# One block of p·v per pair of heads in every second unit, instead of half a block in every unit

## The chip, the core and the metric

One Trainium2 chip, one of its cores. The metric is the device time of one execution in microseconds (us). Each of the core's engines runs its own instructions in order: TensorE (PE, its weight loads apart as PEld), VectorE (DVE), ScalarE (ACT), GpSimd (POOL), and SyncE (SP), which here only issues DMAs. They meet at semaphores.

## What is computed

Attention in which a query sees only the keys of its own hash bucket, then a mixture of experts with a capacity for each expert, then a gated layer behind an RMS norm. The change lies in the attention, here for batch 2, 8 heads, 768 positions and 64 columns:

```python
mask = q_bucket[:, :, :, None] == k_bucket[:, :, None, :]
scores = scale * np.matmul(q, k.transpose(0, 1, 3, 2))
scores = np.where(mask, scores, -1000000000.0)
scores = scores - np.max(scores, axis=-1, keepdims=True)
attn = np.exp(scores)
attn = attn / (np.sum(attn, axis=-1, keepdims=True) + 1e-09)
return np.matmul(attn, v).astype(np.float32)
```

## The kernel before

The attention works on eight pairs of heads (`p`), each pair on six tiles of 128 queries. A block `i` is one tile of one pair; it has two units, u = 2i and u = 2i + 1, one for each head. So a pair takes 12 units, and the whole loop runs over u = 0 to 98, with 96 units of real work. In this text u0 is the first unit of a pair (12, 24, ...), and "relative unit 10" is u0 + 10.

The order is written out by hand, and every engine keeps to it. In unit u:

- `expo(u + 1)`: ACT takes the exponential of a score tile out of PSUM (L342), with the row sum.
- `transp(u)`: PE transposes the exponentials in two halves of three 128x128 pieces (L353); DVE or ACT copies each half to SBUF as `pt` (L357, L355).
- `scores(u + 2)`: four matmuls on PE (L328, L331); DVE then takes the minimum of each row (L333) and makes two scalars of it (L334, L335). The exponential two units on waits for them.
- even u from 4: `comb(i)` on PE (L387) and `comb_v(i)` on DVE (L409 to L416) for the block that was finished in the unit before.
- odd u from 3: `rinv`, three small DVE instructions for the reciprocals of the row sums (L396, L397).
- from u = 2: `pv(u // 2 - 1, u % 2)`. Six matmuls (L372), half of the 12 of a block: chunks 0 to 2 of the keys in the even unit, 3 to 5 in the odd one. Each has 64 columns of weights, one head writing to the upper and one to the lower 64 partitions of `xo`. Behind the second half ACT copies `xo` to SBUF as `xt` (L377), which `comb` reads in the next unit.
- last the `fill` of this unit.

The fill lists prepare the next pair of heads and convert weights for the later layers. For the next pair: `prep_t` (PE transposes, L272; ACT copies, L276 or L278; POOL splits into a high and a low part, L279 and L280) for the halves of k in the fills of relative units -1 and 0, and of q in those of 1 and 3. `prep_d` issues six DMAs on SP for k and six for q, behind the POOL work. `prep_p` (12 matmuls, L288) and `prep_s` (four DMAs, L313) stand in relative unit 7. The scores of the next pair start in relative unit 10.

A weight conversion `conv(n)` stands in relative units 0, 2, 5, 7 and 9: one ACT instruction, two on DVE (L247, L248) and four on POOL (L249 to L252, about 4.5 us of POOL together). Its output `ha` has three buffers, so L247 of one conversion waits until the store of the third before it has landed. The store (`conv_store`, L257) stands on SP four units behind the conversion. So the store of the conversion of relative unit 0 stands on SP behind the `prep_d` of q (relative unit 3), and it frees the buffer that the conversion of relative unit 7 writes.

After the attention come the routing, the experts (layers 1 and 2) and the gated layer. They don't overlap with the attention's loop, apart from weights that are loaded ahead.

Of the kernel before, what the change touches and what calls it, by code (L numbers as in the profile page):

```python
# [9 lines left out]
F32 = mybir.dt.float32  # L10
# [6 lines left out]
AF = mybir.ActivationFunctionType  # L17
# [26 lines left out]
def lsh_attention__moe__swiglu_kernel(ctx, tc, q, k, v, proj, m_wg, m_w1, m_w2,  # L44
                                      f_wg, f_wv, f_wo, f_g, out):
    nc = tc.nc
# [6 lines left out]
    TPB = S // 128  # L53
# [28 lines left out]
    wk = att.enter_context(tc.tile_pool(name="wk", bufs=2))  # L82
    cv = att.enter_context(tc.tile_pool(name="cv", bufs=2))
    ps_s = att.enter_context(tc.tile_pool(name="ps_s", bufs=2, space=PSUM))
    ps_v = att.enter_context(tc.tile_pool(name="ps_v", bufs=1, space=PSUM))
# [229 lines left out]
    SC, PR, PTT, RS, XO = {}, {}, {}, {}, {}  # L315

    def scores(u):
        i, h = divmod(u, 2)
        p, t = divmod(i, TPB)
        k1, k2 = STK["k", p]  # L320
        q1, q2 = STK["q", p]
        if h == 0:
            RS[i] = wk.tile([128, 2, 4], F32, name="rs", bufs=4)
        rs = RS[i]
        ps = ps_s.tile([128, 2, 512], F32, name="sc")
        qs = slice(t * 128, (t + 1) * 128)
        for n in range(2):
            nc.tensor.matmul(ps[:, n, :HALF], q1[:, h, qs], k1[:, h, n * HALF:(n + 1) * HALF],  # L328
                             start=True, stop=False)
        for n in range(2):  # L330
            nc.tensor.matmul(ps[:, n, :HALF], q2[:64 + NS, h, qs], k2[:64 + NS, h, n * HALF:(n + 1) * HALF],  # L331
                             start=False, stop=True)
        nc.vector.tensor_reduce(rs[:, h, 0:1], ps[:, :, :HALF], axis=AX.XY, op=OP.min)  # L333
        nc.vector.tensor_scalar(rs[:, h, 1:2], rs[:, h, 0:1], BIG / 2, -1.0, op0=OP.is_lt, op1=OP.mult)  # L334
        nc.vector.tensor_scalar(rs[:, h, 2:3], rs[:, h, 0:1], BIG / 2, rs[:, h, 0:1], op0=OP.is_lt, op1=OP.mult)  # L335
        SC[u] = ps

    def expo(u):
        i, h = divmod(u, 2)
        rs, ps = RS[i], SC.pop(u)  # L340
        pt = wk.tile([128, 2, HALF], F32, name="pr", bufs=3)
        nc.scalar.activation(pt, ps[:, :, :HALF], AF.Exp, scale=rs[:, h, 1:2], bias=rs[:, h, 2:3],  # L342
                             accum_out=rs[:, h, 3:4])
        PR[u] = pt

    def transp(u):
        pt = PR.pop(u).rearrange("p a b -> p (a b)")
        o = wk.tile([128, TPB, 128], F32, name="pt", bufs=4)
        for half in range(2):
            t = ps_m.tile([128, 512], F32, name="m")[:, :HALF].rearrange("p (c k) -> p c k", c=3)  # L350
            for i in range(3):
                c = half * 3 + i
                nc.tensor.transpose(t[:, i, :], pt[:, c * 128:(c + 1) * 128], ident)  # L353
            if half == 1 or u % 4 < ACT_EVAC:
                nc.scalar.activation(o[:, 3 * half:3 * half + 3, :], t, AF.Copy)  # L355
            else:
                nc.vector.tensor_copy(o[:, 0:3, :], t)  # L357
        PTT[u] = o

    def pv(i, part):  # L360
        p = i // TPB
        vt = LD["v", p]
        if part == 0:
            if i < NU // 2 - 1:
                XO[i] = ps_v.tile([128, 128], F32, name="xo")
            else:
                XO[i] = ps_s.tile([128, 2, 512], F32, name="sc")[:, 0, :128]
        xo = XO[i]
        a = (PTT[2 * i], PTT[2 * i + 1])
        for c in range(3 * part, 3 * part + 3):  # L370
            for h in range(2):
                nc.tensor.matmul(xo[64 * h:64 * h + 64], vt[:, h, c, :], a[h][:, c, :],  # L372
                                 start=(c == 0), stop=(c == TPB - 1))
        if part == 1:
            del PTT[2 * i], PTT[2 * i + 1]
            xt = wk.tile([128, 128], F32, name="xt", bufs=3)
            nc.scalar.activation(xt, xo, AF.Copy)  # L377
            XO[i] = xt

    XS = {}  # L380

# [2 lines left out]
    def comb(i):  # L384
        p, t = divmod(i, TPB)
        pc = ps_m.tile([128, 512], F32, name="m")
        nc.tensor.matmul(pc[:, :2 * W], XO.pop(i), cb[:, p % HP, :], start=True, stop=True)  # L387
        PC[i] = pc
# [3 lines left out]
    def rinv(i):  # L392
        rs = RS.pop(i)
        ri = wk.tile([128, 2, 2], F32, name="ri", bufs=2)
        for h in range(2):
            nc.vector.tensor_scalar(ri[:, h, 0:1], rs[:, h, 3:4], 1e-9, None, op0=OP.add)  # L396
        nc.vector.reciprocal(ri[:, :, 1:2], ri[:, :, 0:1])  # L397
        RI[i] = ri

    def comb_v(i):  # L400
        p, t = divmod(i, TPB)
        b, hp = divmod(p, HP)
        c = b * TPB + t
        ri, pc = RI.pop(i), PC.pop(i)
        if t == 0:
            XS[p] = wk.tile([128, TPB, 2, W], F32, name="xs", bufs=2)
        pcv = pc[:, :2 * W].rearrange("p (h w) -> p h w", h=2)
        if hp == HP - 1:
            nc.vector.tensor_tensor(lp[:, c, 2 * hp:2 * hp + 2, :], pcv[:, :, D:],  # L409
                                    ri[:, :, 1:2].to_broadcast([128, 2, E]), op=OP.mult)  # L410
        if i < NU // 2 - 1:
            nc.vector.tensor_tensor(XS[p][:, t], pcv, ri[:, :, 1:2].to_broadcast([128, 2, W]), op=OP.mult)
        if t == TPB - 1 and hp < HP - 1:
            nc.gpsimd.tensor_copy(lp[:, b * TPB:(b + 1) * TPB, 2 * hp:2 * hp + 2, :], XS[p][:, :, :, D:])
        if hp == HP - 1:
            nc.vector.tensor_reduce(lg[:, c, :], lp[:, c].rearrange("p h e -> p e h"), axis=AX.X, op=OP.add)  # L416
        if i == NU // 2 - 1:
            keys(b)
            for h in range(2):
                nc.scalar.activation(XS[p][:, t, h], pcv[:, h], AF.Copy, scale=ri[:, h, 1:2])  # L420
        if t == TPB - 1:
            for h in range(2):
                nc.sync.dma_start(
                    x_d[b * S:(b + 1) * S, (2 * hp + h) * D:(2 * hp + h + 1) * D].rearrange("(c p) d -> p c d", p=128),
                    XS[p][:, :, h, :D])
            del XS[p]
# [73 lines left out]
    NU = NPAIR * TPB * 2  # L500
# [19 lines left out]
    for n in range(len(convs)):  # L520
        u = CONV + n * 12 // 5
# [71 lines left out]
    for u in range(NU + 3):  # L593

        if u + 1 < NU:
            expo(u + 1)
        if u < NU:
            transp(u)
        if u + 2 < NU:
            scores(u + 2)  # L600
        if u == NU:
            rinv(u // 2 - 1)
            pv(u // 2 - 1, 0)
            pv(u // 2 - 1, 1)
        if u % 2 == 0 and u >= 4:
            comb(u // 2 - 2)
            comb_v(u // 2 - 2)
        if u % 2 == 1 and 3 <= u < NU:
            rinv(u // 2 - 1)
        if 2 <= u < NU:  # L610
            pv(u // 2 - 1, u % 2)
        for f, a in fill.pop(u, []):
            f(*a)
    assert not fill
# [673 lines left out]
```

## Time and profile before

| | us |
|---|---|
| median of three runs | 825.6 (823.95 to 828.76) |
| the profiled execution | 828.43 |
| its span, first to last instruction | 826.3 |
| PE busy over the span | 766.7 |
| the units' loop, first scores to last `comb` | about 16 to 302 |

The loop of units is a third of the time. The granted TensorE clock is given as a share of 2.4 GHz; its mean over the span is 0.961. A time below is a place in the span unless it is plainly a duration.

### The profile page before, as it was taken

What the parts mean: (1) busy time and instruction counts of PE and PEld (TensorE: products, weight loads), DVE (VectorE), ACT (ScalarE), POOL (GpSimd) and SP (SyncE); (2) the same over time, 40 slices, a digit from 0 to 9 for tenths busy, and PEclk for the clock granted to TensorE, in tenths of its full rate; (3) what the DMA queues carried; (4) which work ended last, traced back from release to release, by engine and by line L of the source; (5) the groups of instructions that cost most, each with busy time, mean ns of one, the idle gap of its engine ahead of it and who ended that gap; (6) DMA issues with size and microseconds to landing.
All of it is one profiled execution on the core that took longest, in us unless ns stands there. A gap on an engine that the chain in (4) does not pass through costs nothing.

```text
span 826.3 us, 14742 instructions
## 1 busy us (share of the span) xinstructions
PE 766.7 (93%) x5317; PEld 689.9 (83%) x5317; DVE 524.7 (64%) x1337; ACT 396.5 (48%) x863; POOL 320.9 (39%) x305
## 2 busy tenths in 40 slices
PE   7999989999989973699999998999999999999996
PEld 4788778787877863599988998999999999999995
DVE  7788877888878878478897886665422332233222
ACT  3677666676666770276666764654311211121111
POOL 3287878786777710366665660000100010001001
PEclk7999999999999985699999999999999999999999
DMA  3679989988989424347656824265200110001001
GB/s 77 172 204 232 252 245 242 265 242 240 241 222 256 159 59 128 104 158 260 233 179 196 263 77 130 83 211 151 77 1 1 39 38 1 1 1 39 1 0 39
DMA packets 101744, 113.98 MB, mean 138 GB/s; under 512 B 43820, under 2 KB 74540, under 8 KB 101668
## 3 DMA queue, kind: packets, MB, share of 16 engines
q1 hardware_dynamic: 99588, 106.71, 44.9%
q0 software_dynamic: 1920, 6.29, 2.0%
q8 instruction: 43, 0.70, 0.3%
q14 instruction: 33, 0.27, 0.1%
q10 hardware_dynamic: 160, 0.00, 0.0%
HBM read 76.83 MB, written 18.09 MB: 115 GB/s over the span
## 4 chain that ended last, share of the span: by engine, by line
PE 35%; issue 19%; DVE 2%; DMA 1%; POOL 1%; ACT 1%; SPq 0%; POOLq 0%; another core or an unknown queue 0%; ACTq 0%; DVEq 0%
PE pg L1175 6%; PE pv L1175 6%; PE py L1018 6%; PE po L1203 6%; PE ph L994 5%; PE py L1020 3%; PE ph L996 2%; POOL out_dram L1211 1%; DMA xrow<-x_d,gi 1%; PE ph L972 1%; DMA fraw<-wo_d 1%; DVE wl L212 0%; PE px L1050 0%; DVE yn L1080 0%; DVE xl L954 0%
## 5 line engine op out<-in xcount | busy, mean ns | idle before, releaser
L1211 POOL DMA_INDIRECT out_dram<-ot,oi x12 | 11.7, 975 | 312.3 <-DVE ot L1209 310.6
L342 ACT ACTIVATE pr<-sc,rs 128x768 f32<-128x768 f32 x96 | 95.1, 991 | 61.6 <-DVE rs L335 37.0
L212 POOL TENSOR_TENSOR wl<-wr,wh 128x1024 fp32r<-128x1024 f32 x35 | 84.7, 2428 | 59.3 <-PE ph L972 20.4
L333 DVE TENSOR_REDUCE rs<-sc 128x1 f32<-128x768 f32 x96 | 91.4, 952 | 24.3 <-PE sc L331 24.0
L1184 DVE TENSOR_TENSOR a<-sg,pg 128x384 f32<-128x384 f32 x48 | 26.6, 553 | 103.7 <-ACT sg L1182 103.7
L353 PE MATMUL m<-ident,pr 128*128 128x128 f32 x576 | 84.7, 282 | 6.2 <-ACT pr L342 3.0
L994 PE MATMUL ph<-xg,wh 128*128 128x384 f32 x256 | 78.2, 373 | 8.9 <-DVE ht L1011 8.0
L372 PE MATMUL xo<-pt,ld_v 128*64 128x128 f32 x1128 | 82.8, 282 | 0.0
L353 PEld LDWEIGHTS m<-ident,pr 128*128 128x128 f32 x576 | 62.8, 141 | 20.8 <-issue 6.5
L1018 PE MATMUL py<-ht,wh 128*128 128x384 f32 x256 | 77.2, 365 | 0.0
L372 PEld LDWEIGHTS xo<-pt,ld_v 128*64 128x64 f32 x1128 | 60.0, 137 | 18.6 <-issue 11.9
L1182 ACT ACTIVATE sg<-pg 128x384 f32<-128x384 f32 x48 | 23.5, 489 | 106.2 <-PE pg L1175 106.2
L1188 ACT ACTIVATE ah<-a 128x384 fp32r<-128x384 f32 x48 | 25.2, 525 | 99.0 <-DVE a L1185 99.0
L1175 PE MATMUL pg<-xh,gl 128*128 128x384 f32 x192 | 64.6, 336 | 0.0
L1175 PE MATMUL pg<-xl,gh 128*128 128x384 f32 x192 | 64.5, 336 | 0.0
L1175 PE MATMUL pg<-xh,gh 128*128 128x384 f32 x192 | 64.5, 336 | 0.0
L1175 PE MATMUL pv<-xh,vl 128*128 128x384 f32 x192 | 64.4, 335 | 0.0
L1175 PE MATMUL pv<-xl,vh 128*128 128x384 f32 x192 | 64.4, 335 | 0.0
L1175 PE MATMUL pv<-xh,vh 128*128 128x384 f32 x192 | 64.4, 335 | 0.0
L1020 PE MATMUL py<-ht,wl 128*128 128x192 f32 x256 | 64.0, 255 | 0.0
L355 ACT ACTIVATE pt<-m 128x384 f32<-128x384 f32 x120 | 55.6, 485 | 5.2 <-PE m L353 5.2
L328 PE MATMUL sc<-s_k,s_q 128*128 128x384 f32 x192 | 57.9, 383 | 0.0
(252 smaller groups left out, 1963.0 us busy)
## 6 DMA issues: line engine op xcount, KB each, us to landing
wr<-in_moe_w_dram SPq DMA_DIRECT2D x64, 512.0 KB
w<-in_moe_w_gate_dram SPq DMA_DIRECT2D x12, 512.0 KB
w<-in_moe_w_val_dram SPq DMA_DIRECT2D x12, 512.0 KB
w<-in_moe_w_out_dram SPq DMA_DIRECT2D x12, 512.0 KB
s_k<-nh_k SPq DMA_DIRECT2D x28, 192.0 KB
s_q<-nh_q SPq DMA_DIRECT2D x28, 192.0 KB
ld_k<-in_k_dram SPq DMA_DIRECT2D x16, 192.0 KB
ld_q<-in_q_dram SPq DMA_DIRECT2D x16, 192.0 KB
```

What stands on the lines that cost most here:

```text
L212: (nc.gpsimd if pool else nc.vector).tensor_tensor(WL[i], WR.pop(i), WH[i], op=OP.subtract)
L328: nc.tensor.matmul(ps[:, n, :HALF], q1[:, h, qs], k1[:, h, n * HALF:(n + 1) * HALF], start=True, stop=False)
L333: nc.vector.tensor_reduce(rs[:, h, 0:1], ps[:, :, :HALF], axis=AX.XY, op=OP.min)
L342: nc.scalar.activation(pt, ps[:, :, :HALF], AF.Exp, scale=rs[:, h, 1:2], bias=rs[:, h, 2:3], accum_out=rs[:, h, 3:4])
L353: nc.tensor.transpose(t[:, i, :], pt[:, c * 128:(c + 1) * 128], ident)
L355: nc.scalar.activation(o[:, 3 * half:3 * half + 3, :], t, AF.Copy)
L372: nc.tensor.matmul(xo[64 * h:64 * h + 64], vt[:, h, c, :], a[h][:, c, :], start=(c == 0), stop=(c == TPB - 1))
L994: hi = lambda: nc.tensor.matmul(ph[:, :2 * CAP], wh[:, d], xg[:, d].rearrange("p a b -> p (a b)"), start=(d == 0), stop=(d == KD - 1), ski ...
L1018: hi = lambda: nc.tensor.matmul(py[d][:, :2 * CAP], wh[:, ds], ht[:, f].rearrange("p a b -> p (a b)"), start=(f == 0), stop=(f == KF - 1), ...
L1020: lo = lambda: nc.tensor.matmul(py[d][:, :CAP], wl[:, ds], ht[:, f, 0], start=False, stop=False, skip_group_check=True)
L1175: nc.tensor.matmul(t[:, :TJ], a[:, d, :], b_[:, d, :], start=(n == 0), stop=(n == 3 * KD - 1))
L1203: nc.tensor.matmul(PO[j][t], a[:, ts], b_, start=(f == 0 and n == 0), stop=(f == KG - 1 and n == 2))
```

## The change

A whole block of `pv` (12 matmuls) now runs in every even unit, behind the scores and `comb`; an odd unit has none. The copy `xt` becomes a function of its own, `pv_out`, and runs in the odd unit behind it, on ACT between the exponential and the copies of the transposes. `rinv` moves from the odd to the even unit. The last block runs in u = 96 behind `comb(46)`, where it ran ahead of it. Behind the changed lines all line numbers are smaller by one to four.

```diff
-    def pv(i, part):
+    def pv(i):
...
-        a = (PTT[2 * i], PTT[2 * i + 1])
-        for c in range(3 * part, 3 * part + 3):
+        a = (PTT.pop(2 * i), PTT.pop(2 * i + 1))
+        for c in range(TPB):
             for h in range(2):
                 nc.tensor.matmul(xo[64 * h:64 * h + 64], vt[:, h, c, :], a[h][:, c, :],
                                  start=(c == 0), stop=(c == TPB - 1))
-        if part == 1:
-            del PTT[2 * i], PTT[2 * i + 1]
-            xt = wk.tile([128, 128], F32, name="xt", bufs=3)
-            nc.scalar.activation(xt, xo, AF.Copy)
-            XO[i] = xt
+
+    def pv_out(i):
+        xt = wk.tile([128, 128], F32, name="xt", bufs=3)
+        nc.scalar.activation(xt, XO[i], AF.Copy)
+        XO[i] = xt
...
         if u + 1 < NU:
             expo(u + 1)
+        if u % 2 == 1 and 3 <= u <= NU + 1:
+            pv_out(u // 2 - 1)
         if u < NU:
             transp(u)
         if u + 2 < NU:
             scores(u + 2)
-        if u == NU:
-            rinv(u // 2 - 1)
-            pv(u // 2 - 1, 0)
-            pv(u // 2 - 1, 1)
         if u % 2 == 0 and u >= 4:
             comb(u // 2 - 2)
             comb_v(u // 2 - 2)
-        if u % 2 == 1 and 3 <= u < NU:
+        if u % 2 == 0 and 2 <= u <= NU:
+            pv(u // 2 - 1)
             rinv(u // 2 - 1)
-        if 2 <= u < NU:
-            pv(u // 2 - 1, u % 2)
         for f, a in fill.pop(u, []):
             f(*a)
```

On PE, relative units -1 and 0 of a pair in the middle of the loop, where the next pair's k is transposed (`ld_k`), stand so in the kernel before:

```order
L353 MATMUL m<-ident,pr 128x128 x6
L328 MATMUL sc<-s_k,s_q 128x384 x2
L331 MATMUL sc<-s_k,s_q 128x384 x2
L372 MATMUL xo<-pt,ld_v 64x128 x6
L272 MATMUL m<-ident,ld_k 128x128 x3
L353 MATMUL m<-ident,pr 128x128 x6
L328 MATMUL sc<-s_k,s_q 128x384 x2
L331 MATMUL sc<-s_k,s_q 128x384 x2
L387 MATMUL m<-cb,xt 128x144
L372 MATMUL xo<-pt,ld_v 64x128 x6
L272 MATMUL m<-ident,ld_k 128x128 x3
```

and so in the changed one:

```order
L353 MATMUL m<-ident,pr 128x128 x6
L328 MATMUL sc<-s_k,s_q 128x384 x2
L331 MATMUL sc<-s_k,s_q 128x384 x2
L272 MATMUL m<-ident,ld_k 128x128 x3
L353 MATMUL m<-ident,pr 128x128 x6
L328 MATMUL sc<-s_k,s_q 128x384 x2
L331 MATMUL sc<-s_k,s_q 128x384 x2
L386 MATMUL m<-cb,xt 128x144
L371 MATMUL xo<-pt,ld_v 64x128 x12
L272 MATMUL m<-ident,ld_k 128x128 x3
```

The half block ahead of the first L272 is gone, and the second L272 (the second half of k) stands behind a whole block where it stood behind half of one.

At the end of the loop, PE has in the kernel before (the last block writes to a buffer of `sc`):

```order
L353 MATMUL m<-ident,pr 128x128 x6
L372 MATMUL xo<-pt,ld_v 64x128 x6
L372 MATMUL sc<-pt,ld_v 64x128 x12
L387 MATMUL m<-cb,xt 128x144 x2
L690 LDWEIGHTS reach
```

and in the changed one:

```order
L353 MATMUL m<-ident,pr 128x128 x6
L386 MATMUL m<-cb,xt 128x144
L371 MATMUL sc<-pt,ld_v 64x128 x12
L386 MATMUL m<-cb,xt 128x144
L686 LDWEIGHTS reach
```

Between the last transposes and the last block stands one `comb` now, where half a block of `pv` stood. The order of the DMAs on SP and of the work on POOL is the same in both kernels.

## Rows read from the trace of the kernel before

**Rows 1.** The page: busy time by engine; granted clock in 40 slices.

```profile
PE 766.7 (93%) x5317; PEld 689.9 (83%) x5317; DVE 524.7 (64%) x1337; ACT 396.5 (48%) x863; POOL 320.9 (39%) x305
...
PEclk7999999999999985699999999999999999999999
```

**Rows 2.** Window: length, busy us of PE, PEld, DVE, ACT, POOL; clock, DMA share, GB/s.

```profile
30.00:298.00 268.00, 255.28 (x2295) 215.03 (x2294) 220.72 (x647) 183.94 (x410) 195.61 (x202) 0.99 0.83 228
```

**Rows 3.** Waits in 30 to 305 us: total us, times, longest.

```profile
PE sc L331 <- issue: 4.4, 2, 2.2
```

**Rows 4.** PE in order of time (start, length), units 43 to 45; end of loop.

```profile
151.91 0.82 PE L353 MATMUL m<-ident,pr 128*128 128x128 f32 x6
152.49 0.59 PE L328 MATMUL sc<-s_k,s_q 128*128 128x384 f32 x2
...
153.26 0.41 PE L387 MATMUL m<-cb,xt 128*128 128x144 f32 x2
153.60 0.88 PE L372 MATMUL xo<-pt,ld_v 128*64 128x128 f32 x12
154.41 0.88 PE L353 MATMUL m<-ident,pr 128*128 128x128 f32 x6
155.04 0.59 PE L328 MATMUL sc<-s_k,s_q 128*128 128x384 f32 x2
...
155.92 0.88 PE L372 MATMUL xo<-pt,ld_v 128*64 128x128 f32 x12
...
297.56 0.88 PE L353 MATMUL m<-ident,pr 128*128 128x128 f32 x6
298.36 0.88 PE L372 MATMUL xo<-pt,ld_v 128*64 128x128 f32 x12
299.07 1.48 PE L372 MATMUL sc<-pt,ld_v 128*64 128x128 f32 x24
300.48 1.02 PE L387 MATMUL m<-cb,xt 128*128 128x144 f32 x4
```

**Rows 5.** In order of time, units 36 to 46 of one pair.

```profile
132.29 0.50 POOL L279 CAST nh_k<-nr_k 128x384 fp32r<-128x384 f32 x1 [1.30 <-ACT nr_k L278]
...
145.25 1.01 POOL L280 TENSOR_TENSOR nl_q<-nr_q,nh_q 128x384 fp32r<-128x384 f32 x1
...
149.93 0.59 SPq L257 DMA_DIRECT2D wv_d<-ha  x1
...
154.91 0.43 DVE L247 TENSOR_SCALAR ha<-w 128x512 int32<-128x512 int32 x1 [2.12 <-DMA wv_d<-ha]
...
156.96 0.99 ACT L342 ACTIVATE pr<-sc,rs 128x768 f32<-128x768 f32 x1 [3.65 <-DVE lp L409]
...
158.10 0.87 PE L353 MATMUL m<-ident,pr 128*128 128x128 f32 x6 [1.30 <-ACT pr L342]
...
158.31 0.28 ACT L377 ACTIVATE xt<-xo 128x128 f32<-128x128 f32 x1
```

**Rows 6.** The same two ends for the first and last of six such pairs.

```profile
60.74 0.50 POOL L279 CAST nh_k<-nr_k 128x384 fp32r<-128x384 f32 x1 [1.31 <-ACT nr_k L278]
...
85.53 0.88 PE L353 MATMUL m<-ident,pr 128*128 128x128 f32 x6 [0.29 <-ACT pr L342]
...
240.93 0.50 POOL L279 CAST nh_k<-nr_k 128x384 fp32r<-128x384 f32 x1 [1.30 <-ACT nr_k L278]
...
265.83 0.33 PE L353 MATMUL m<-ident,pr 128*128 128x128 f32 x1 [0.40 <-ACT pr L342]
```

**Rows 7.** PE in order of time, units 23 and 34.

```profile
91.51 0.52 PE L272 MATMUL m<-ident,ld_k 128*128 128x128 f32 x3 [0.91 <-DVE rs L335]
...
124.40 0.58 PE L331 MATMUL sc<-s_k,s_q 82*128 82x384 f32 x2 [2.18 <-issue]
```

**Rows 8.** Stretches of units 34 to 35 and 70 to 71; columns as in rows 2.

```profile
120.99:128.66 7.67, 5.49 (x50) 4.47 (x50) 5.14 (x17) 4.15 (x10) 6.09 (x6) 1.00 1.06 214
228.03:237.30 9.27, 7.08 (x50) 5.88 (x50) 5.24 (x17) 4.26 (x10) 6.08 (x6) 0.82 1.08 265
```

More of the change, by code (lines that the diff above doesn't have):

```diff
@@ L358, in transp @@
         PTT[u] = o
-    def pv(i, part):
+    def pv(i):
         p = i // TPB
         vt = LD["v", p]
[L363 to L367, printed above, removed]
+        if i < NU // 2 - 1:
+            XO[i] = ps_v.tile([128, 128], F32, name="xo")
+        else:
+            XO[i] = ps_s.tile([128, 2, 512], F32, name="sc")[:, 0, :128]
         xo = XO[i]
-        a = (PTT[2 * i], PTT[2 * i + 1])
-        for c in range(3 * part, 3 * part + 3):
+        a = (PTT.pop(2 * i), PTT.pop(2 * i + 1))
+        for c in range(TPB):
             for h in range(2):
```

## The prediction

> **What bounds the kernel now.** I read the page first. PE is the busiest engine by far [rows 1], and in the loop of units it is busy for 255.3 of 268.0 us [rows 2]. That says "PE-bound", and a change that takes work off PE would pay in full. But the table of that stretch has four near rivals: DVE at 82%, POOL at 73%, ACT at 69%, and the DMA engines at 83%. So I looked next at where PE's 12.7 us of idle time lie, with the list of waits and the order of time. They are not spread out. They come back at the same places of each pair: at the transposes of relative unit 10, which wait for an exponential [rows 5, 6], and in two pairs at the scores of the next pair in the same unit, 2.2 us each [rows 3, 7].
>
> Then I followed one of these waits back [rows 5]. The transposes of unit 46 start at 158.10, right behind their exponential (156.96). ACT had been idle for 3.65 us before that. The row names DVE, and what DVE was late with is the row above: the conversion of relative unit 7 stood 2.12 us at the head of DVE's queue until the store from 149.93 had landed, at 154.91. The row minimum for unit 46 was queued behind it. That store stands on SP behind the six DMAs of q, which wait for POOL's last low part of q (145.25 + 1.01 = 146.26). POOL had started on the second half of k at 132.29 and had worked from there on without a pause (high and low part of k, two conversions, two times q). And it had been idle for 1.30 us before 132.29, waiting for that half of k. So the chain is: PE transposes the second half of k in relative unit 0, then 14.0 us of POOL, 3.7 us of SP, 5.0 us of landing, 3.2 us of DVE and ACT, and then relative unit 10, 25.8 us after its start. In the first and the last pair of this kind it takes 85.53 - 60.74 = 24.8 us and 265.83 - 240.93 = 24.9 us [rows 6]. There are six such pairs, all between 24.8 and 25.8, and in each PE waits at the end. **From the second half of k to relative unit 10, PE is not the bound; it waits for 0.3 to 1.3 us.** Only the stretch from relative unit 10 to the next pair's second half of k, some 2.5 units, and both ends of the loop are PE's own.
>
> **What the change takes off PE.** Times from start to start [rows 4]. (Each of these matmuls leaves two records, so half a block is x12.) From scores to a `pv` block it takes 155.92 - 155.04 = 0.88 us, from scores to `comb` 153.26 - 152.49 = 0.77: going over to weights of 64 columns costs 0.11. Half a block takes 154.41 - 153.60 = 0.81; the whole block at the end takes 300.48 - 299.07 = 1.41, without the way in. Transposes behind a block take 0.63, behind other work 152.49 - 151.91 = 0.58. So one block less saves 0.11 + (2 x 0.81 - 1.41) + 0.05 = 0.37 at most; less the way in, which the 1.41 lacks, I take 0.3. There are 95 blocks before (94 halves and the whole one at the end), 48 after: 47 x 0.3 = 14 us of PE time.
>
> The Trainium skill, "TensorEngine Tiling (Array Packing)", Tiling Modes, Key Properties, says that a change of tiling mode drains the engine. The 0.11 agrees; taken alone, the rule makes this change a gain of those 14 us.
>
> **Where it goes.** In the new order an even unit costs 0.58 + 0.77 + (153.60 - 153.26) + 1.45 (the 1.41 with a way in) = 3.14 and an odd one 0.63 + 0.77 = 1.40, where they cost 2.55 and 2.32 [rows 4]. Between the second half of k and relative unit 10 lie five odd and four even units: 5 x 0.92 - 4 x 0.59 = 2.2 us less of PE. The chain of POOL, SP, DMA and DVE over the same stretch holds nothing that the change touches: the order on POOL and SP is the same, and PE's own work for it (q) comes earlier, while POOL is still busy with what stands ahead. So these 2.2 us become a longer wait: 2.5 us in place of 0.3, up to 3.5 in place of 1.3. **Gain in this stretch: none.**
>
> From relative unit 10 to the next second half of k, before: 2.55 + 2.32 + the part of unit u0 up to that half, 2.55. After: 3.14 + 1.40 + 3.14. That is 0.3 us *more*, since the half of k now stands behind a whole block. Where a wait for DVE lies between (0.91 us in unit 23 [rows 7]) the shorter odd unit helps nothing and it is 0.6. The 2.2 us wait at the next pair's scores [rows 7] is for DMAs that SP issues behind the same store; I leave it as it is (if it shrank, at most 4.4 us in all would come back [rows 3]). Five such intervals: 1.5 to 3.0, taken as 2.2.
>
> At the start, up to the first chain in unit 12, PE has no wait in its way: five pairs of units by 0.3, less the half block (0.6) that now stands ahead: -0.9. At the end, behind the last chain (unit 82), six pairs by 0.3 less the half block in unit 82 itself: -1.2. Of the last half block nothing comes back: before, the last block starts 299.07 - 297.56 = 1.5 us behind the last transposes, which `comb` and the copies fill as well.
>
> The rest costs nothing on the path. `pv_out` (0.28 us [rows 5]) now stands on ACT ahead of a copy of transposes, behind an exponential of 0.99 us during which its block gets done; and ACT is idle for 31% of the loop. If that cover were gone it would be 0.28 in each of 48 blocks, 13 us; I take nothing. `rinv` moves by one unit, its sum unchanged.
>
> Sum: -0.9 + 2.2 - 1.2 = +0.1 us (from -0.6 to +0.9).
>
> **The clock.** Longer waits have a price of their own. Two stretches start with relative unit 10 and have the same PE work, 50 rows each, and the same idle time in them, 7.67 - 5.49 and 9.27 - 7.08 = 2.2 us [rows 8]. In one the granted clock is 1.00 and it takes 7.67 us; in the other it fell to the lower level (1.2 GHz) for a while, mean 0.82, and it takes 9.27. So a fall costs 1.6 us, and behind 2.2 us of idle PE it came once in two times. After the change each of the six pairs waits 2.5 us or more at relative unit 10; in the pair of rows 5 it is 3.5 at one go, and in that of unit 34 the 2.2 us of [rows 7] follow shortly behind. I take these two as falls that were not there: +3.2. Bounds: none, or five more (+8).
>
> The Trainium skill, "TensorE: Matmul & The Clock Gate", HAM oscillation, tells of a kernel that waited for a DMA in each tile and paid the fall each time. By that rule it would be all of them.
>
> Together +3.3 us against the profiled execution's 828.43. That one lay 2.8 us above the median of the runs, so I put the difference on the median: 825.6 + 3.3 = 828.9, say **829.0 us**.
>
> **Rivals.** A measurement of this kernel tells about 0.5% from no change, 4.1 us.
>
> 1. *The chain gives way and PE's saving comes through.* For it: PE is at 95%, and 11 of the 25.8 us are SP, DMA and DVE, which may shift. If half comes through, 7 us, 818.6; all of it, 811.6. Against it: in all six pairs the transposes start with the end of their exponential, and POOL's 14 us have no pause. Chance 0.16.
> 2. *The clock falls in every pair.* Place: the transposes of relative unit 10 and what follows. Price 1.6 each; from three further falls on (4.8 + 0.1 > 4.1) it is slower by the bound above. All five more: 825.6 + 8.1 = 833.7. For it: one of two waits of 2.2 us led to it already. Against it: where DVE is behind anyhow, as in unit 23, a slower PE costs less. Chance 0.38 for three or more.
> 3. *That the blocks are not joined* is out: the order shows 12 in a row.
>
> My forecast, chain holds and at most two more falls: 0.46. That makes faster 0.16, same 0.46, slower 0.38. The range goes from half the saving that comes through, with a fall or two more (820), to five falls and the upper sum (835); it leaves out full gains and anything beyond, below 2 in 10. The likeliest case by itself: 825 to 830.
>
> **What would show it.** Right: in the changed profile `xo` matmuls come 24 rows in a go in even units, and PE's busy time in the loop falls by about 14 us while the loop ends within 4 us of where it did. PE's waits at relative unit 10 grow to 2.5 us and more, with POOL's start on the second half of k still 24.8 to 25.8 us ahead. The clock's low slices in the loop are more than one. Wrong: these waits stay below 1 us and the distance from POOL's start to unit 10 shrinks to about 23 us. Then the chain was PE's after all, and rival 1 holds. If the distance grows, say by a `pv_out` that holds ACT up or by a later landing, it is slower than the sum, and the place is where the chain's steps got longer.

## The result, and the profile after

The changed kernel takes 831.48 us (median of 20 runs, 826.78 to 838.2), the kernel before 828.02 (20 runs, 820.77 to 833.49): a ratio of 1.0059, interval 1.0036 to 1.0081 (the two medians alone give 1.0042). It is slower, by 3.5 us between the medians where 3.4 were forecast, inside the range. The forecast called up to 0.5% no change; the interval reaches to both sides of that, so whether the loss is larger is not settled. The profiled execution took 832.48 us, its span 830.3.

From the page of the changed kernel, its busy times and the clock by slices:

```profile
PE 762.2 (92%) x5317; PEld 694.4 (84%) x5317; DVE 524.6 (63%) x1337; ACT 394.1 (47%) x863; POOL 321.2 (39%) x305
...
PEclk7999998999999995599999999999999999999999
```

The window of [rows 2] in the changed kernel, same columns:

```profile
30.00:298.00 268.00, 246.35 (x2262) 216.59 (x2263) 217.37 (x638) 179.05 (x404) 195.62 (x202) 0.98 0.83 228
```

PE is now idle for 268.00 - 246.35 = 21.7 us of this window, where it was 12.7, and the loop still ends later. From the first scores to the last transposes, before and after:

```profile
15.25:297.56 282.31, 267.90 (x2361) 224.32 (x2359) 230.69 (x668) 192.06 (x428) 198.59 (x206) 0.99 0.80 218
15.24:302.02 286.78, 263.41 (x2373) 229.73 (x2371) 230.62 (x671) 189.89 (x428) 198.60 (x206) 0.98 0.78 215
```

PE's busy time fell by 4.5 us, not by 14. Where nothing waits, the units do cost what was forecast. PE in order of time, from the block of unit 28 to the start of unit 31 in the changed kernel:

```profile
105.39 1.53 PE L371 MATMUL xo<-pt,ld_v 128*64 128x128 f32 x24
106.85 0.88 PE L353 MATMUL m<-ident,pr 128*128 128x128 f32 x6
...
108.27 0.82 PE L353 MATMUL m<-ident,pr 128*128 128x128 f32 x6
...
109.62 0.41 PE L386 MATMUL m<-cb,xt 128*128 128x144 f32 x2
109.96 1.53 PE L371 MATMUL xo<-pt,ld_v 128*64 128x128 f32 x24
111.72 0.52 PE L353 MATMUL m<-ident,pr 128*128 128x128 f32 x3 [0.23 <-DVE pt L357]
```

An odd unit takes 108.27 - 106.85 = 1.42 us (forecast 1.40). The even one would take 3.15 (forecast 3.14): 109.96 - 108.27 and 106.85 - 105.39 = 1.46 for the block. What it takes is 111.72 - 108.27 = 3.45, for at its end PE waits for a copy of DVE. Waits of PE for DVE's copies are new in the loop.

The chain of [rows 5], in the same pair:

```profile
135.91 0.51 POOL L279 CAST nh_k<-nr_k 128x384 fp32r<-128x384 f32 x1 [1.96 <-ACT nr_k L278]
...
148.87 1.00 POOL L280 TENSOR_TENSOR nl_q<-nr_q,nh_q 128x384 fp32r<-128x384 f32 x1
...
153.15 0.81 SPq L257 DMA_DIRECT2D wv_d<-ha  x1
...
157.47 0.43 DVE L247 TENSOR_SCALAR ha<-w 128x512 int32<-128x512 int32 x1 [1.72 <-DMA wv_d<-ha]
...
159.52 0.99 ACT L342 ACTIVATE pr<-sc,rs 128x768 f32<-128x768 f32 x1 [2.99 <-DVE lp L408]
...
160.66 0.33 PE L353 MATMUL m<-ident,pr 128*128 128x128 f32 x1 [0.99 <-DVE pt L357]
```

24.8 us from start to end (25.8 before). The two ends in the first and last of the six pairs, to be laid beside [rows 6], and PE's first matmul behind the loop:

```profile
61.27 0.51 POOL L279 CAST nh_k<-nr_k 128x384 fp32r<-128x384 f32 x1 [1.62 <-ACT nr_k L278]
...
86.05 0.33 PE L353 MATMUL m<-ident,pr 128*128 128x128 f32 x1 [1.27 <-ACT pr L342]
...
245.35 0.51 POOL L279 CAST nh_k<-nr_k 128x384 fp32r<-128x384 f32 x1 [1.95 <-ACT nr_k L278]
...
270.05 0.33 PE L353 MATMUL m<-ident,pr 128*128 128x128 f32 x1 [1.21 <-ACT pr L342]
...
309.00 0.86 PE L686 MATMUL prank<-oh,reach 128*128 128x8 bf16 x12 [3.38 <-DVE reach L678]
```

That matmul in the kernel before:

```profile
304.87 0.32 PE L690 MATMUL prank<-oh,reach 128*128 128x8 bf16 x3 [3.37 <-DVE reach L682]
```

The chains took 24.78 and 24.70 us. The sums over the six chains, in the view of windows, before and after:

```profile
sum 150.94, PE 145.31 PEld 122.04 DVE 125.65 ACT 103.67 POOL 121.11; mean PE 24.22 PEld 20.34 DVE 20.94 ACT 17.28 POOL 20.18
sum 149.49, PE 135.87 PEld 119.94 DVE 122.55 ACT 101.89 POOL 121.00; mean PE 22.64 PEld 19.99 DVE 20.43 ACT 16.98 POOL 20.17
```

**The chain kept its length, 24.9 us for 25.2 in the mean, while PE's busy time alongside it fell by 1.6 us in each pair (2.2 were forecast).** The waits of PE at the end of these two chains grew from 0.29 and 0.40 to 1.27 and 1.21.

The stretches of [rows 8], in the view of windows of the changed kernel:

```profile
121.24:131.60 10.36, 7.53 (x49) 6.60 (x50) 4.53 (x15) 4.35 (x10) 6.09 (x6) 0.67 1.02 242
231.66:241.06 9.40, 6.77 (x49) 5.88 (x50) 4.52 (x15) 4.34 (x10) 6.08 (x6) 0.82 1.11 255
```

PE in the first of them, in order of time:

```profile
121.24 0.87 PE L353 MATMUL m<-ident,pr 128*128 128x128 f32 x6 [1.23 <-ACT pr L342]
...
125.30 0.98 PE L331 MATMUL sc<-s_k,s_q 82*128 82x384 f32 x2 [2.82 <-DMA s_k<-sg]
```

In the pair of unit 34 the clock fell now, where it had not; in that of unit 70 it fell as before. The first stretch took 10.36 - 7.67 = 2.7 us longer; 0.6 of that is the longer wait (2.82 for 2.18).

So the loop's end moved by 309.00 - 304.87 = 4.1 us: 0.5 up to the first chain, 2.7 in the stretch of unit 34, 1.0 in the other pairs (270.05 - 265.83 = 4.2 less those two), -0.1 behind the last chain. Behind the loop these two profiled executions take the same time, 521.4 us; those of the runs below take 517.0 (e3) to 523.0 (e4) there. So single executions are compared by places in the loop, not by their spans.

### The profile page after: what moved, and what is told of

The parts are those of the page before. It is cut to its first block, busy times and chain, and to the rows that moved or that the text cites. A ratio compares the mean times of both kernels' runs of the same rounds, so it can differ in the third digit from the quotient of the medians.

```text
span 830.3 us, 14700 instructions
## 1 busy us (share of the span) xinstructions
PE 762.2 (92%) x5317; PEld 694.4 (84%) x5317; DVE 524.6 (63%) x1337; ACT 394.1 (47%) x863; POOL 321.2 (39%) x305
## 4 chain that ended last, share of the span: by engine, by line
PE 35%; issue 19%; DVE 2%; DMA 1%; POOL 1%; ACT 1%; SPq 0%; POOLq 0%; another core or an unknown queue 0%; ACTq 0%; DVEq 0%
PE pg L1171 6%; PE pv L1171 6%; PE py L1014 6%; PE po L1199 6%; PE ph L990 5%; PE py L1016 3%; PE ph L992 2%; POOL out_dram L1207 1%; DMA xrow<-x_d,gi 1%; PE ph L968 1%; DMA fraw<-wv_d 1%; DVE wl L212 0%; PE px L1046 0%; DVE yn L1076 0%; DVE xl L950 0%
## 5 line engine op out<-in xcount | busy, mean ns | idle before, releaser
L371 PE MATMUL xo<-pt,ld_v 128*64 128x128 f32 x1128 | 74.6, 283 | 0.0
L1184 ACT ACTIVATE ah<-a 128x384 fp32r<-128x384 f32 x48 | 25.2, 525 | 100.0 <-DVE a L1181 100.0
L371 PEld LDWEIGHTS xo<-pt,ld_v 128*64 128x64 f32 x1128 | 62.9, 140 | 7.1 <-issue 0.8
```

## Experiments

**Theory A** is that of the forecast: the second half of the next pair's k starts a chain of fixed length, and only PE work ahead of that half counts. **Rival B**: PE bounds the loop, and the saving is worth less than its rows, or lost to the clock's falls. All ratios are to the kernel before.

**Move only the half of k** ahead of the block, or move the block to the odd units.

```diff
 # e1, on the changed kernel
+        if u % 12 == 0 and u > 0:
+            early = [x for x in fill.get(u, []) if x[0] is prep_t]
+            fill[u] = [x for x in fill.get(u, []) if x[0] is not prep_t]
+            for f, x in early:
+                f(*x)
         if u % 2 == 0 and 2 <= u <= NU:
             pv(u // 2 - 1)
 # e2, on the changed kernel
-        if u % 2 == 1 and 3 <= u <= NU + 1:
+        if u % 2 == 0 and 4 <= u <= NU:
+            pv_out(u // 2 - 2)
+        if u == NU + 1:
             pv_out(u // 2 - 1)
...
-        if u % 2 == 0 and 2 <= u <= NU:
-            pv(u // 2 - 1)
-            rinv(u // 2 - 1)
+        if u % 2 == 1 and 3 <= u < NU or u == NU:
+            i = u // 2 - 1
+            pv(i)
+            rinv(i)
```

> The changed kernel, but in relative unit 0 the transposes of the second half of the next pair's k stand ahead of the whole block of p*v, no longer behind it. Theory A (the chain from that half of k through POOL, SP, DMA and DVE to relative unit 10 is fixed, and the block in front of it delays its start): the chain starts up to 1.45 us earlier in each of six pairs, so 4 to 8 us faster than the changed kernel (1.0059 of the kernel before), that is 0.996 to 1.001 of the kernel before; the distance from POOL's start on that half to the transposes of unit 10 stays at 24.7 to 25.3 us. Rival B (the loss is the clock's, which falls in the longer waits; the place of the block doesn't matter): the waits get longer still, so 1.006 or more.

> The changed kernel with the whole block in the odd units (behind the scores) and its copy in the following even unit, so that no block stands ahead of the second half of k. Theory A: the stretch of PE from unit 10 to that half falls from 7.68 to about 6.4 us, where it was 7.42 before; 5 to 7 us faster than the kernel before if nothing else binds there, 0.992 to 0.998 of it. Rival B: as many falls of the clock as in the changed kernel or more, 1.004 to 1.010.

Measured: e1 1.0031 (0.9998 to 1.0065), e2 1.0016 (0.9989 to 1.0043). Both medians lie below the changed kernel's, as A has it, but the intervals overlap its own, and e2's lies wholly above the 0.992 to 0.998 that A expected. Inconclusive, for each edit brought a wait of its own. From e1's list of PE's waits (sum, number, longest):

```profile
PE m L272 <- ACT pt L355: 5.1, 6, 1.0
```

The same from e2's:

```profile
PE m L386 <- ACT xt L376: 12.0, 23, 1.7
```

In e1 the transposes of the second half of k wait for a copy of ACT in each of the six pairs; in its profile the gain of the earlier start (60.33 for 61.27) was gone by the next pair, where the clock fell at 87 us and the scores of the next pair waited. In e2 `comb` waits for its copy `xt`, which now stands in the same unit.

**Take the DMA out of the chain**: five buffers for the converted weights.

```diff
-        ha = cv.tile([128, 512], I32, name="ha", bufs=3)
+        ha = cv.tile([128, 512], I32, name="ha", bufs=5)
```

> The kernel before, with five buffers for the converted weights in place of three: the conversion of relative unit 7 then no longer waits for the store of relative unit 0. Theory A: the wait of DVE for that store goes, and with it the waits of PE at relative unit 10 (0.05 to 1.3 us in six pairs, with what they hide about 3.8 in all): 2 to 4 us faster, 0.995 to 0.998. Rival B: the same, since the waits in front of the one fall of the clock get shorter.

> The changed kernel with five buffers for the converted weights. Theory A: with the chain cut at its DMA, the saving of PE (14 us of switches) can come through where it was waited away: 8 to 12 us faster than the changed kernel, 0.991 to 0.996 of the kernel before and faster than the kernel before with five buffers. Rival B (the switches saved are not worth what the records say, and the rest is the clock): it gains over the changed kernel only what five buffers give the kernel before, 1.002 to 1.004. Rival C (DVE binds next to the chain): it comes out like the kernel before with five buffers, 0.995 to 0.998.

Measured: e3 0.9971 (0.9939 to 1.0004), e4 1.005 (1.0021 to 1.0078). e3 is as expected. A expected 0.991 to 0.996 of e4, so as it stood it failed here; B's 1.002 to 1.004 lies inside e4's interval. In both, the wait of DVE for the store is gone and unit 10 no longer waits: the chain to it takes 23.3 us in e4 (24.5 in e3). But e4 loses it again within the same unit. The list of waits of PE at the next pair's scores, changed kernel:

```profile
PE sc L331 <- DMA s_k<-sg: 2.8, 1, 2.8
PE sc L331 <- issue: 2.6, 1, 2.6
...
PE sc L331 <- DMA s_q<-sg: 0.4, 1, 0.4
```

The same list for e4:

```profile
PE sc L331 <- issue: 8.5, 2, 4.3
PE sc L331 <- DMA s_q<-sg: 5.3, 4, 2.2
```

And e4's PE in order of time, in the pair of rows 5:

```profile
157.49 0.82 PE L353 MATMUL m<-ident,pr 128*128 128x128 f32 x6
158.06 0.59 PE L328 MATMUL sc<-s_k,s_q 128*128 128x384 f32 x2
160.46 0.58 PE L331 MATMUL sc<-s_k,s_q 82*128 82x384 f32 x2 [1.80 <-DMA s_q<-sg]
```

The scores of the next pair wait for its sign bits (`s_q<-sg`) in every pair now: 13.8 us in all, against 5.8. Those come over SP behind the same DMAs of q, so their chain too starts at the second half of k: in e4 these scores stand 25.0 to 28.8 us behind it, in the kernel before 25.9 to 28.9, in the changed one 25.8 to 29.3. **Two chains start at that half of k and end a fraction of a unit apart; cutting one shows the other.** I call this theory A'.

**Give PE work back, inside the chains and ahead of them.** In `scores(u)`, before its first matmul:

```diff
 # e5: units 1, 3, 5, 7, 9 of each of the six pairs
+        for _ in range(2 if 12 <= u - 2 < 84 and (u - 2) % 12 in (1, 3, 5, 7, 9) else 0):
+            nc.tensor.matmul(ps[:, 0], ones_w, ones_w.unsqueeze(1).to_broadcast([128, 4, 128]), start=True, stop=True)
 # e6: the same with 5 in units 11 and 0
+        for _ in range(5 if 11 <= u - 2 < 84 and (u - 2) % 12 in (11, 0) else 0):
```

> The changed kernel with ten extra matmuls on ones (512 columns, bf16, about 0.22 us each, into the score tile that is written next) in each of the six pairs, two in each odd unit from relative unit 1 to 9: 13 us more work for PE, just where it is said to have 2 us to give. Theory A (the chains that start at the second half of k decide when relative unit 10 and the next pair's scores can run): the time stays within 2 us of the changed kernel, 1.004 to 1.008 of the kernel before. Rival B (PE bounds this stretch): 13 us more, about 1.021. Rival C (the clock's falls are the loss, and more work in the waits holds the clock up): 2 to 4 us faster than the changed kernel, 1.001 to 1.004.

> The changed kernel with the same extra matmuls, five each in relative units 11 and 0, ahead of the next pair's second half of k (65 in all, about 14 us). Theory A: PE is on the path there, except where DVE is behind anyhow; 7 to 13 us slower than the changed kernel, 1.014 to 1.022 of the kernel before. Rival D (a DMA limit over the whole pair, so that no place on PE matters): within 3 us of the changed kernel, 1.004 to 1.010.

Measured: e5 1.0047 (1.0017 to 1.0076), median 832.09; e6 1.0212 (1.0164 to 1.0261), median 846.07, 14.6 us above the changed kernel. The same matmuls are nearly free inside the chains (0.6 us in the median; in e5's profiled execution the first matmul behind the loop stands at 311.50, 2.5 us later, of 12 put in) and cost time ahead of them, as A has it and neither B nor a limit over the whole pair allows. The half of k that starts the chain (POOL) and the transposes at its end (PE) in e5, first and last pair:

```profile
60.72 0.50 POOL L279 CAST nh_k<-nr_k 128x384 fp32r<-128x384 f32 x1 [1.63 <-ACT nr_k L278]
85.40 0.33 PE L355 MATMUL m<-ident,pr 128*128 128x128 f32 x1 [0.21 <-ACT pr L344]
...
246.75 0.51 POOL L279 CAST nh_k<-nr_k 128x384 fp32r<-128x384 f32 x1 [1.96 <-ACT nr_k L278]
272.62 0.33 PE L355 MATMUL m<-ident,pr 128*128 128x128 f32 x1 [1.48 <-ACT pr L344]
```

The same two in e6's first pair:

```profile
62.68 0.51 POOL L279 CAST nh_k<-nr_k 128x384 fp32r<-128x384 f32 x1 [3.04 <-ACT nr_k L278]
87.47 0.33 PE L355 MATMUL m<-ident,pr 128*128 128x128 f32 x1 [1.30 <-ACT pr L344]
```

24.7 and 25.9 us in e5, 24.8 in e6. In e5 the wait at unit 10 shrank to 0.21 in the first pair: the extra work fills it.

Not all of e6's 14.6 us is the time of its matmuls. From relative unit 10 to the next half of k there are five stretches. The first and the third in the changed kernel:

```profile
86.05:96.01 9.96, 9.91 (x95) 8.42 (x96) 7.91 (x24) 6.90 (x17) 7.58 (x8) 1.00 1.01 264
...
160.66:170.61 9.95, 9.60 (x95) 8.47 (x96) 9.09 (x31) 6.93 (x17) 7.56 (x8) 1.00 1.06 315
```

The same two in e6:

```profile
87.46:98.89 11.43, 11.43 (x105) 9.74 (x106) 8.90 (x27) 7.01 (x17) 7.61 (x8) 1.00 0.96 277
...
166.48:181.47 14.99, 14.55 (x105) 12.10 (x106) 9.37 (x31) 7.24 (x17) 7.59 (x8) 0.77 0.75 207
```

With the clock at 1.00 in both kernels, the ten matmuls (about 2 us) cost 1.5 us; in the third stretch the clock fell in e6 alone, and it is 5.0 us longer. So some 9 of the 14.6 us are the matmuls' own (six times 1.5, an estimate), and the rest went along with falls.

**Ease both chains**: five buffers, and the loads of the experts' weights moved behind the six pairs.

```diff
-        at(20 + i * 9, load_w, i)
+        at(84 + i, load_w, i)
```

> The kernel before with five buffers for the converted weights, and with the eight loads of the experts' weights (512 KB each) in units 84 to 91 in place of every ninth unit from 20: they no longer stand in the DMA queue ahead of the sign bits which the next pair's scores wait for. With five buffers alone PE waited 2.6 and 3.2 us for them in the two pairs that have such a load in relative unit 5. Theory A' (the second chain, through the landing of the sign bits, starts at the same half of k): these waits go, 4 to 6 us faster than with five buffers alone, 0.990 to 0.993 of the kernel before. Rival D (bytes over the whole loop bind): the same gain or more. Rival B (PE bounds): nothing beyond five buffers, 0.996 to 0.999.

> The changed kernel with both. With five buffers alone PE waited for the sign bits in all six pairs (0.6, 4.3, 1.8, 0.6, 4.3, 2.2 us). Theory A': the two long waits shrink to the size of the others, 5 to 8 us faster than the changed kernel with five buffers; 0.995 to 0.999 of the kernel before, still behind the kernel before with both edits, since the second half of k stands behind a whole block and the chain from it is still the longer one. Rival B (PE bounds once the DMAs are out of the way): faster than the kernel before with both edits, by up to 14 us, 0.978 to 0.985.

Measured: e7 0.9862 (0.9822 to 0.9901), e8 0.9952 (0.9917 to 0.9987). e8 is as expected; e7 gains more than the 0.990 to 0.993 of A'. With its waits the falls of the clock went too: in the window of rows 2 the clock is 1.00 in e7 and 0.98 in e3. Rival D would allow e7's gain as well; against it stands e6. Both kernels gain, and the changed one falls further behind, as A' says: with both edits the kernel before hardly waits for a chain, and the changed one still does in all six pairs, since its half of k comes later and its PE comes sooner. The list of PE's waits at the next pair's scores in e7:

```profile
PE sc L331 <- DMA s_q<-sg: 0.5, 1, 0.5
PE sc L331 <- issue: 0.2, 1, 0.2
```

The same in e8:

```profile
PE sc L331 <- DMA s_q<-sg: 9.6, 6, 2.6
```

**Start the chains earlier**, in the odd unit that has no block any more.

```diff
-SLOTS = (-1, 0, 1, 3, 7, 7)
+SLOTS = (-1, -1, 1, 3, 7, 7)
```

e9 has it on top of e8's edits, e10 on top of e7's, e11 alone on the changed kernel.

> The changed kernel with five buffers and late loads (0.9952 of the kernel before), and both halves of the next pair's k transposed in relative unit -1, which has no block of p*v any more, in place of -1 and 0. Theory A' (both chains start at the second half of k, so what stands ahead of it on PE is paid in full): it stands some 2.5 us earlier on PE; POOL, which is still at work on the conversion of relative unit 9, lets it start 1 to 2.5 us earlier. 6 to 12 us faster, 0.980 to 0.988 of the kernel before, and level with or ahead of the kernel before with the same two DMA edits (0.986). Rival D (bytes or POOL's sum over the pair bind): within 3 us of 0.995.

> The same move of the half of k in the kernel before with five buffers and late loads (0.9862). Theory A': there PE waits for neither chain at relative unit 10 any more (except 0.2 and 0.5 us in two pairs), so an earlier start has nothing to give: within 2 us of it, 0.984 to 0.989. If this one gains as much as e9, the chain is not what tells the two kernels apart.

> The changed kernel with the move of the half of k alone (three buffers, loads as they were). Theory A': 4 to 9 us faster than the changed kernel, 0.995 to 1.001 of the kernel before, less whatever the longer waits cost in falls of the clock. Rival B (PE bounds, the place of the half of k does not matter): 1.004 to 1.008, as the changed kernel.

Measured: e9 0.9819 (0.9769 to 0.9869), e10 0.9801 (0.9759 to 0.9844), e11 0.9998 (0.9962 to 1.0035). e9 and e11 came out as A' has it: 12 us (median 812.01 for 824.21) and 4.6 us (826.91 for 831.48) from the place of three transposes, where a PE-bound loop gives nothing. e10 did not: 5.1 us (811.21 for 816.33), where I expected at most 2, though its interval overlaps that of e7. Its trace has lost other waits than those of the chains. In e7 the transposes waited for copies of ACT, six times in relative unit 5; in e10 once. The row of e7's list of waits:

```profile
PE m L353 <- ACT pt L355: 2.6, 6, 0.4
```

And of e10's:

```profile
PE m L353 <- ACT pt L355: 0.4, 1, 0.4
```

PE's waits in the loop are shorter by 4.5 us in all: 2.2 here, 1.0 at the transposes of k, 0.7 at the next pair's scores, 0.6 at the copy of k in unit 60. That these make up the gain is an inference. e9 and e10 are the fastest versions, level with each other: the changed order lost its handicap, but the 14 us of PE that it was to save have not come through there either. In e9's profiled execution (819.75 us, the slowest of its six runs) PE waits for 9.4 us in all at the next pair's scores, where e10's trace has no such wait, and the clock is low in three places; whether the faster runs of e9 have less of both, no trace shows.

**Hold the clock up** where it fell.

```diff
 # in scores(u), before its first matmul
+        for _ in range(10 if u in (36, 72) else 0):
+            nc.tensor.matmul(ps[:, 0], ones_w, ones_w.unsqueeze(1).to_broadcast([128, 4, 128]), start=True, stop=True)
```

> The changed kernel with ten matmuls on ones (about 2.2 us) ahead of the scores in units 34 and 70, where PE waits 2.8 and 2.6 us for the sign bits behind a wait of 1.2 and 1.6 us, and where the clock fell in the profiled execution. If these falls are a good part of the loss: no fall there, 3 to 4 us faster than the changed kernel, 1.001 to 1.003 of the kernel before. If they are not: 1.004 to 1.008, as the changed kernel.

Measured: 1.003 (0.999 to 1.007), median 827.98. The estimate lies where the falls would explain 2.5 to 3.5 us, but its interval reaches the changed kernel's 1.0059. The profile is plainer. The two stretches of rows 8 in e12, with the ten extra matmuls in them:

```profile
121.70:129.60 7.90, 7.36 (x60) 5.62 (x61) 4.54 (x15) 4.12 (x10) 6.08 (x6) 1.00 1.13 224
229.55:236.91 7.36, 7.35 (x60) 5.61 (x60) 4.74 (x15) 4.13 (x10) 6.10 (x6) 1.00 1.09 244
```

No fall in either, 7.90 us for 10.36 and 7.36 for 9.40. More PE work in the same wait, and the stretch is over 2 us sooner. PE's first matmul behind the loop stands at 304.69, 4.3 us before the changed kernel's and level with the 304.87 of the kernel before, which has one fall.

## Why the prediction was right, and where it was off

*The saving is real but not on the path.* Right in kind: units of 1.42 and 3.15 us, and e5 shows that some 12 us of PE time (60 matmuls of about 0.2 us) can be put back inside the chains for little. Too large in size: 14 us were forecast off PE's busy time in the loop, and 4.5 came. Some 2 us went back in the stretch of unit 34 alone, at the lower clock (busy for 7.53 us, where it was 5.49). What became of the rest is open; busy time counts each matmul to a modelled end, so part of a short wait behind it counts as busy.

*The chain is fixed.* Right in the six pairs: 24.7 to 25.2 us after, 24.8 to 25.8 before. It was incomplete: I had one chain and left the second, to the next pair's scores, "as it is". It starts at the same half of k, so the forecast held; but e4 would have been forecast wrongly, and was. And "in each PE waits at the end" was too strong: in the pair of unit 58 the kernel before had no wait of PE there that the trace lists.

*The waits at relative unit 10 grow to 2.5 us and more.* Wrong: 0.7 to 1.6 in the six pairs. The step that failed is "so these 2.2 us become a longer wait". By the sums over the six chains PE's busy time fell by 1.6 us a pair; its idle time grew by 1.3 (150.94 - 145.31 = 5.6 in all, then 149.49 - 135.87 = 13.6), and the chains took 0.2 less. Nor was it waited away in one place, but along the chain, too: at exponentials and copies in relative units 2, 4 and 7 (the 0.23 above is one). PE's waits at transposes in the loop came to 14.1 us (8.4 for exponentials, 5.7 for copies), where they were 6.1.

*Start, -0.9.* Wrong: +0.5 (60.74 to 61.27). I took PE as unhindered there. It was, in the old order; in the new one its weight loads wait in units 4 and 5 (0.35 us each) and its transposes in unit 12 (0.28). By unit 12 it had gained 0.4 us where 1.5 (five times 0.3) were counted (its transposes start at 56.69 for 57.10), and unit 12 lost 0.9 where 0.6 were counted. *End, -1.2.* Wrong too: -0.1 (265.83 to 304.87, 270.05 to 309.00); the list of waits gains some at units 86 and 92.

*From unit 10 to the next half of k, +2.2 over five intervals.* Right. The sums over the five, before and after:

```profile
sum 54.10, PE 47.47 PEld 40.17 DVE 41.66 ACT 34.64 POOL 37.52; mean PE 9.49 PEld 8.03 DVE 8.33 ACT 6.93 POOL 7.50
sum 59.24, PE 52.56 PEld 45.83 DVE 43.72 ACT 35.31 POOL 37.53; mean PE 10.51 PEld 9.17 DVE 8.74 ACT 7.06 POOL 7.51
```

That is +5.1, and +2.4 without the 2.7 of the stretch of unit 34. The chains, put at no change, gave 1.4 us back (150.9 to 149.5), most of it in the pair of rows 5.

*The clock, two more falls at 1.6.* One more, in the pair of unit 34 where it was expected, longer than the one of unit 70: 2.7 us with a scores' wait of 2.82 for 2.18. None in the pair of rows 5, where 3.5 us of wait were forecast and about 1 came.

So the loop's +4.1 is 0.5 - 1.4 + 2.4 + 2.7 - 0.1, where the forecast's +3.3 was -0.9 + 0 + 2.2 + 3.2 - 1.2. Two savings of about 1 us each did not come, and one fall fewer and the shorter chains made up for most of that. That the total came within 0.1 us of the medians' difference is luck; that the saving would not come through is not.

*Rival 1* (the chain gives way) is out, by rows 6's answers and by e5. *Rival 2* (a fall in every pair) did not come in this execution; that falls cost is borne out by e12's stretches. In the mean over runs, too, the changed kernel has the lower clock: 0.957 over its 20 runs, 0.962 over the 81 runs of the kernel before that stand beside the experiments. Within its 20 runs a clock lower by 0.01 goes with 4.8 us more (a fitted line), so by estimate some 2 of the 3.5 us are falls.

## What to carry to other kernels

A stage in which PE is busy for 95% can still be paced by a chain through other engines: look at where the last 5% lie, and if they come back at one place, measure the distance from there to the instruction that started the chain, period by period. If it is constant, work saved inside is worth next to nothing, and work that lands ahead of the start is paid for; a few idle matmuls put in either place show it in one run each, if the granted clock is compared beside the time. And a block that is merged to save overhead also moves what is queued behind it: see first whether the start of such a chain is among that.

## What the runs showed of the hardware

Extra matmuls made a stretch faster: 2 us of matmuls on ones in front of a wait kept the granted clock at 1.00, and the stretch took 7.90 us in place of 10.36 (e12).

A transfer of 54 KB (the sign bits) can be late by 3 us through a load of 512 KB that nothing in the loop waits for. In the two pairs with such a load in relative unit 5, the scores waited 2.6 and 3.2 us in e3; with the loads moved away, in e7, no wait is listed there, at nearly the same traffic over the loop (230 GB/s for 228).
